# Top-k attention and a mixture-of-depths layer on one core: a software pipeline in another order

## The chip, the cores and the metric

The kernel runs on one core of one Trainium2 chip. The metric is the device time of one execution in microseconds. Five engines work side by side, each through its own list of instructions in order, and wait for each other by semaphores: TensorE (PE; its weight loads are PEld), VectorE (DVE), ScalarE (ACT), GpSimd (POOL) and SyncE (SP), which here only issues DMAs.

## What is computed

For 8 batches and 8 heads, 576 queries attend to 576 keys, but only to those whose score reaches the 32nd largest of the row. The result, 576 rows of 512 numbers per batch, is the input of the second part: the 128 rows with the largest gate pass through a small two-layer network and are added back.

```python
def _attn_ref(q, k, v):                      # (8, 8, 576, 64)
    scores = scale * np.matmul(q, k.transpose(0, 1, 3, 2))
    kth = np.partition(scores, -32, axis=-1)[..., -32:-31]
    scores = np.where(scores >= kth, scores, -1e9)
    attn = softmax(scores)
    return np.matmul(attn, v)

def _moe_ref(x, w_gate, w1, w2, capacity):   # x (8, 576, 512), capacity 128
    scores = np.einsum('bsd,d->bs', x, w_gate)
    out = x.copy()
    for b in range(B):
        top_idx = np.argpartition(-scores[b], capacity)[:capacity]
        xe = x[b, top_idx]
        ye = np.maximum(xe @ w1, 0.0) @ w2
        g = 1.0 / (1.0 + np.exp(-scores[b, top_idx]))
        out[b, top_idx] = x[b, top_idx] + g[:, None] * ye
    return out
```

## The kernel before

All is fp32. The work is cut into 160 units: 8 batches, 5 query tiles `t` (four of 128 rows, one of 64) and 4 head pairs `hp`. A unit of t=0 to 3 has two score tiles of 128 x 576, one per head; a unit of t=4 has one, with the 64 rows of both heads. One turn of the main loop, a step `n`, works on several units at once, each at another stage. The step's place within its batch is called i (n mod 20) below.

For a unit u the stages are these. In step u-1 TensorE multiplies its scores into PSUM (`multiply`, tile `ps`) and ScalarE copies them to `sc` (`keep`). In step u VectorE finds a lower bound of the 32nd score (`find_bound`: 16 maxima of eight over pieces, tile `cand`, then three rounds, tiles `best`), and ScalarE cuts it to a shorter number (`cut`, tile `seen`). In step u+1 ScalarE takes the Sign of score against bound (`part`, tile `sides`, with a count), POOL multiplies score and Sign and appends a few steps that depend on the count (`y`, `fill`), and VectorE finds the exact 32nd score in `y` (`find_kth`, tile `next8`, printed as `next`). In step u+2 the mask `less` is made, for the first tile by ScalarE, for the second by POOL. In step u+3 TensorE turns scores and adds a large negative number where the mask is set (`turn` into `ptr`, `turn_last` for the last 64 keys into a corner of the step's `ps`), and ScalarE takes exponentials (`pT`, `last`). In step u+4 TensorE multiplies with the values (`values`, tile `av`; the last column sums the weights) and ScalarE copies that out (`keep_values`, tile `xs`). Every fourth unit ends a query tile: VectorE inverts the sums (`invert`), one step later POOL normalises (`normalise`) and VectorE makes the gate (`gates`).

Two generators are moved on by one part at the end of each step. `load_kq` fetches and turns the keys and queries of the next batch (tile `tr`, its copies wait in `late` until the next `flush`). `mixture` is the second layer for the batch before: from i=4 on two steps turn the gates, five rank the rows by a comparison with all (`junk`) and mark which row has which slot (`pick`), one multiplies the marks with row number and gate (`extra_ps`), one gathers the 128 rows by DMA, then come their turning, three steps of products with w1 (`h_ps`), four with w2 (`y_ps`) and a scatter that adds. `ps_misc`, one PSUM bank, holds whatever of these is in flight.

What sets the order is the program's own text: the wrapper `InOrder` (lines 34 to 42) keeps each engine's instructions as they are written. `ps` has one buffer of four banks, `ptr` two of one, `av` and `ps_misc` one each. Because `turn_last` and the next score product share a `ps` buffer, that product follows the exponential of `last` (line 764) on ScalarE.

Of the kernel before, what the change touches and what calls it, by code (L numbers as in the profile page):

```python
# [10 lines left out]
ALU = mybir.AluOpType  # L11
# [34 lines left out]
def kernel(  # L46
# [50 lines left out]
    nc.gpsimd.iota(tok_i[:, J:NT], pattern=[[0, 1]], base=JP, channel_multiplier=1)  # L97
    slot_i = const.tile([P, CAP], I32, name="slot_i")
    nc.gpsimd.iota(slot_i, pattern=[[1, CAP]], base=0, channel_multiplier=0)
    slot = const.tile([P, CAP], FP32, name="slot")  # L100
# [391 lines left out]
    def mixture(row0, gate, rank, exact=False):  # L492
# [23 lines left out]
        extra = modpool.tile([P, NT, 2], FP32, name="extra")  # L516
        sig = modpool.tile([P, NT], FP32, name="sig")
        parts = ((slice(0, P), slice(0, J)), (slice(0, R), slice(J, NT)))
        for n, t in parts:
            dve.tensor_scalar_add(  # L520
                out=extra[n, t, 0],
                in0=tok_i[n, t],
                scalar1=row0 if isinstance(row0, float) else row0[n, :],
            )

            dve.tensor_scalar_max(out=sig[n, t], in0=gate[n, t], scalar1=-88.0)
        late.append(
            lambda: [
                act.activation(sig[n, t], sig[n, t], AF.Exp, scale=-1.0)
                for n, t in parts  # L530
            ]
        )


        pick = modpool.tile([P, NT, CAP], FP32, name="pick")
        for t in range(NT):
            yield
            n = R if t == J else P
            junk = modpool.tile([P, S], FP32, name="junk", tag="scratch")
            dve.tensor_scalar(  # L540
                out=junk[0:n, :],
                in0=gate_row[0:n, :],
                scalar1=gate[0:n, t : t + 1],
                scalar2=None,
                op0=ALU.is_gt,
                op1=ALU.add,
                accum_out=rank[0:n, t : t + 1],
            )
# [9 lines left out]
            if t == 0:  # L558
                for n, t in parts:
                    dve.tensor_scalar_add(out=sig[n, t], in0=sig[n, t], scalar1=1.0)  # L560
                    dve.reciprocal(out=extra[n, t, 1], in_=sig[n, t])

        yield
        ps = ps_misc.tile([P, 512], FP32, name="extra_ps", tag="misc")
# [12 lines left out]
        yield  # L577
        row_i = modpool.tile([P, 1], I32, name="row_i", bufs=2)
        done = B if exact else int(row0) // S + 1

        dve.tensor_scalar_min(out=row_i, in0=picked[:, 0:1], scalar1=float(done * S - 1))
# [21 lines left out]

        hT = modpool.tile([P, NFC, CAP], FP32, name="hT")
        for f0 in range(0, NFC, 3):
            yield
            fcs = range(f0, min(f0 + 3, NFC))
# [18 lines left out]
        for fc in range(NFC):  # L626
# [9 lines left out]
            lambda ps=ps: act.activation(gy, ps, AF.Copy, scale=picked[:, 1:2])  # L636
# [11 lines left out]
    def gates(t, x, gate):  # L648
        n = R if t == J else P
        prod = modpool.tile([P, S], FP32, name="prod", tag="scratch")  # L650
        dve.tensor_tensor_reduce(
            out=prod[0:n, 0:HD],
            in0=x[0:n, t, :],
            in1=wg[0:n, :],
            scale=1.0,
            scalar=0.0,
            op0=ALU.mult,
            op1=ALU.add,
            accum_out=gate[0:n, t : t + 1],
        )  # L660

# [14 lines left out]
    load_at = (3, 6, 7, 8, 9, 10, 12, 13, 14)  # L676
    first_load_at = (5, 6, 7, 8, 9, 10, 11, 12, 13)
    load_steps = {}
    for b in range(B - 1):
        at = [b * per_batch + i for i in (load_at if b else first_load_at)]  # L680
# [17 lines left out]
    scs, bests, next8s, masks, weights = {}, {}, {}, {}, {}  # L698
# [4 lines left out]
    for n in range(-1, len(units) + 6):  # L703
# [19 lines left out]
        if tiles_of(n - 3):  # L723
            sc, less, trs = scs.pop(n - 3), masks.pop(n - 3), []
            pT = ptpool.tile([P, 2, J, P], FP32, name="pT")
            last = ptpool.tile([P, P], FP32, name="last")
        if tiles_of(n - 4):
            b4, t4, hp4 = units[n - 4]
            av = ps_av.tile([P, 512], FP32, name="av")
        if tiles_of(n - 3) or tiles_of(n + 1):  # L730
            ps = room_for_scores()
        for i in range(2):
            if i < tiles_of(n - 3):
                trs.append(turn(i, sc, less))
                if i == tiles_of(n - 3) - 1:
                    trs.append(turn_last(i + 1, sc, ps, less))
            if i < tiles_of(n - 4):
                values(t4, hp4, i, *weights[n - 4], av, qkv[b4][2])


        if tiles_of(n):
            bests[n] = find_bound(tiles_of(n), scs[n])


        if tiles_of(n - 1):
            sides = wkpool.tile([P, 2, S], BF16, name="sides")
            y = wkpool.tile([P, 2, S + 8], FP32, name="y")
            for i in range(tiles_of(n - 1)):
                part(i, scs[n - 1], first_tile[n - 1], sides)
                pool.tensor_tensor(  # L750
                    y[:, i, 0:S], scs[n - 1][:, i, :], sides[:, i, :], ALU.mult
                )
            fill(tiles_of(n - 1), y, first_tile[n - 1])
            next8s[n - 1] = find_kth(tiles_of(n - 1), y)
        if tiles_of(n - 3):
            w = tiles_of(n - 3)
# [7 lines left out]
            act.activation(last[0 : w * R, :], trs[w], AF.Exp, scale=scale)  # L764
            weights[n - 3] = pT, last
        flush()
        if tiles_of(n + 1):
            b, t, hp = units[n + 1]
            multiply(t, hp, *qkv[b][0:2], ps)
        if tiles_of(n - 2):  # L770
            w, at = tiles_of(n - 2), first_tile[n - 2]
            kth = next8s.pop(n - 2)
            masks[n - 2] = mask(w, scs[n - 2], kth)
            pool.tensor_copy(out=seen[:, 1, at : at + w], in_=kth[:, 0:w, 7])
        if tiles_of(n - 4):
# [6 lines left out]
            weights.pop(n - 4)  # L782
            keep_values(t4, hp4, av, xs)
        if tiles_of(n + 1):
            scs[n + 1] = keep(tiles_of(n + 1), ps)
        if tiles_of(n):
            cut(tiles_of(n), bests.pop(n), first_tile[n])
# [13 lines left out]
        if b > 0 and i == mix_at:  # L801
# [13 lines left out]
    for _ in mixing:  # L815
        flush()
# [142 lines left out]
```

## Time and profile before

| | |
|---|---|
| median of 3 runs | 1075.84 us (1075.49 to 1076.65) |
| profiled execution | 1080.1 us, its span 1077.9 us |
| busy share of the span: TensorE, VectorE, ScalarE, POOL | 93%, 79%, 74%, 66% |
| mean granted clock of TensorE | 0.931 |
| chain that ended last, by engine | PE 62%, DVE 21%, ACT 9%, POOL 5% |

The profile is one execution. The granted clock is a share of 2.4 GHz; 0.50 is 1.2 GHz. A row of waits names who waited, and behind the arrow what ended the wait. The helper's line (L42) stands for nearly all instructions, so groups are told apart by their tiles.

### The profile page before, as it was taken

Reading aid. Unit: us, or ns where it says so; the run is one execution under the profiler, and the core shown is the slowest. Engines: PE = TensorE matmul, PEld = TensorE weight load, DVE = VectorE, ACT = ScalarE, POOL = GpSimd, SP = SyncE. Lnnn points to the kernel's source line nnn. Section 1 sums busy time; section 2 is a strip of 40 time slices with the busy share of each in tenths; the row PEclk is TensorE's granted clock in tenths of the full one; section 3 lists DMA queues with packets and bytes.
Section 4 is the critical chain, followed back from the end, with each engine's and each line's share of the span. In section 5 each row is a group of like instructions: output and inputs, shape, how many; then the busy total and the mean of one; then the engine's idle time right before and its main releaser. Section 6 shows DMA issues by size and latency. Waiting matters only on the chain.

```text
span 1077.9 us, 24886 instructions
## 1 busy us (share of the span) xinstructions
PE 1002.5 (93%) x7962; PEld 810.6 (75%) x7962; DVE 850.9 (79%) x4981; ACT 797.4 (74%) x1961; POOL 707.5 (66%) x814
## 2 busy tenths in 40 slices
PE   5899989999899999999999998999989999889966
PEld 3688778786778867787777877878677886777844
DVE  4999898868898689985888869896889858897440
ACT  4899788777787678885886868887788767777510
POOL 3788587664786557883776838786578655787410
PEclk9999999799897999899987999899989799888978
DMA  5741104100241003310131102320024000100020
GB/s 115 227 104 35 40 7 94 45 11 2 58 105 40 1 2 94 70 40 2 55 79 40 31 2 55 89 50 11 2 60 94 11 2 2 55 1 12 2 63 13
DMA packets 123834, 49.13 MB, mean 46 GB/s; under 512 B 118960, under 2 KB 118960, under 8 KB 122672
## 3 DMA queue, kind: packets, MB, share of 16 engines
q1 hardware_dynamic: 120320, 42.88, 15.5%
q0 software_dynamic: 1792, 4.20, 2.3%
q8 instruction: 65, 1.06, 0.4%
q14 instruction: 73, 0.60, 0.2%
q10 hardware_dynamic: 1584, 0.39, 0.2%
HBM read 35.91 MB, written 11.53 MB: 44 GB/s over the span
## 4 chain that ended last, share of the span: by engine, by line
PE 62%; DVE 21%; ACT 9%; POOL 5%; issue 2%; DMA 1%; SPq 0%; ACTq 0%; POOLq 0%
PE av L42 19%; PE ps L42 15%; PE ptr L42 12%; DVE cand L42 10%; PE h_ps L42 6%; PE y_ps L42 6%; DVE next L42 5%; POOL y L42 4%; ACT sides L42 3%; DVE best L42 2%; ACT sc L42 2%; PE tr L42 2%; DVE junk L42 2%; ACT pT L42 2%; PE extra_ps L42 1%
## 5 line engine op out<-in xcount | busy, mean ns | idle before, releaser
L42 POOL TENSOR_TENSOR y<-sc,sides 128x576 f32<-128x576 f32 x288 | 366.6, 1292 | 293.0 <-ACT sides L42 293.0
L42 DVE MAX8 cand<-sc 128x8 f32<-128x72 f32 x2304 | 323.8, 216 | 131.4 <-ACT sc L42 131.4
L42 PE MATMUL av<-v,pT 128*128 128x65 f32 (+1 forms) x2560 | 328.7, 274 | 0.0
L42 PEld LDWEIGHTS av<-v,pT 128*128 128x128 f32 (+1 forms) x2560 | 299.4, 189 | 8.4 <-issue 1.7
L42 PE MATMUL ps<-kT,qT 64*128 64x288 f32 (+1 forms) x1280 | 218.6, 464 | 29.0 <-ACT last L42 24.4
L42 PE MATMUL ptr<-ident,sc 128*128 128x128 f32 x1152 | 242.3, 290 | 0.0
L42 DVE MAX8 next<-y 128x8 f32<-128x584 f32 x288 | 207.3, 757 | 41.9 <-POOL y L42 38.9
L42 ACT COPY sc<-ps 128x576 f32<-128x576 f32 x288 | 172.0, 644 | 83.7 <-PE ps L42 81.9
L42 ACT ACTIVATE sides<-sc,seen 128x576 bf16<-128x576 f32 x288 | 221.2, 769 | 15.2 <-POOL seen L42 0.4
L42 ACT ACTIVATE pT<-ptr 128x512 f32<-128x512 f32 x288 | 159.1, 583 | 95.5 <-PE ptr L42 95.4
L42 PE MATMUL ptr<-out_of_reach,less 128*128 128x128 bf16 x1152 | 221.6, 226 | 1.9 <-POOL less L42 1.9
L42 POOL TENSOR_SCALAR less<-sc,next 128x576 bf16<-128x576 f32 x128 | 220.8, 1725 | 0.0
L42 PEld LDWEIGHTS ptr<-ident,sc 128*128 128x128 f32 x1152 | 175.6, 152 | 31.1 <-issue 16.2
L42 PEld LDWEIGHTS ps<-kT,qT 64*128 64x128 f32 (+1 forms) x1280 | 113.3, 192 | 78.5 <-ACT last L42 42.6
L42 DVE MAX8 best<-cand 128x8 f32<-128x64 f32 x864 | 154.2, 215 | 3.3
L42 PEld LDWEIGHTS <-less 128*128 128x128 bf16 (+1 forms) x1312 | 141.5, 108 | 15.1 <-issue 7.5
L42 ACT ACTIVATE less<-sc,next 128x576 bf16<-128x576 f32 x160 | 125.5, 784 | 0.0
L42 DVE MATCH_REPLACE8 cand<-best,cand 128x64 f32<-128x64 f32 x576 | 116.5, 209 | 0.0
L42 PEld LDWEIGHTS h_ps<-xeT,w 128*128 128x128 f32 x512 | 60.6, 196 | 11.8 <-ACT xs L42 9.2
L42 PE MATMUL h_ps<-xeT,w 128*128 128x128 f32 x512 | 65.2, 284 | 1.8 <-ACT hT L42 1.2
L42 PE MATMUL y_ps<-w,hT 128*128 128x512 f32 x128 | 62.6, 615 | 0.5 <-ACT hT L42 0.5
L42 ACT COPY xs<-av 128x130 f32<-128x130 f32 (+1 forms) x160 | 43.7, 273 | 24.2 <-PE av L42 24.1
(78 smaller groups left out, 919.6 us busy)
## 6 DMA issues: line engine op xcount, KB each, us to landing
rows<-in_k_dram SPq DMA_DIRECT2D x64, 128.0 KB, 2.9
v<-in_v_dram SPq DMA_DIRECT2D x64, 128.0 KB, 3.0
out_dram<-x SPq DMA_DIRECT2D x8, 1024.0 KB, 3.9
rows<-in_q_dram SPq DMA_DIRECT2D x62, 128.0 KB, 2.9
w<-in_moe_w_dram SPq DMA_DIRECT2D x2, 2048.0 KB, 14.1
last<-in_k_dram SPq DMA_DIRECT2D x8, 128.0 KB, 3.4
vlast<-in_v_dram SPq DMA_DIRECT2D x8, 128.0 KB, 3.3
vpair<-in_v_dram SPq DMA_DIRECT2D x16, 64.0 KB, 2.8
```

Of the source, the lines that this page charges most:

```text
L42: return lambda *a, **kw: self._tc.keep_in_program_order(fn(*a, **kw))
```

## The change

The order of a step is rewritten, and the second layer moves.

In a step `n`, TensorE first turns unit n-4, `last` before the two tiles, then multiplies the scores of n+1, then the values of n-4. ScalarE first takes the exponentials of n-4 (`last` first), then the loads' copies, the mask of n-3, the copies of the scores of n+1, the cut and the Signs of n-1, and the copy of the values at the end. VectorE finds the bound of n and then the 32nd score of n-2, whose `y` was made in the step before. Mask and turning thus come one step later for a unit; the values come at the step where they were.

On ScalarE a step with a load reads so before; the tiles are those named above, `kT` the loaded keys:

```order
L42 ACTIVATE sides,seen<-sc,seen 128x576 x2
L42 ACTIVATE pT<-ptr 128x512 x2
L42 ACTIVATE last<-ps 128x128
L42 COPY kT<-tr 128x512
L42 ACTIVATE less<-sc,next_6841 128x576
L42 COPY xs<-av 128x130
L42 COPY sc<-ps 128x576 x2
L42 CAST seen<-best_6908 128x2
```

and so after, from the exponentials of one step to the next step's first:

```order
L42 ACTIVATE last<-ps 128x128
L42 ACTIVATE pT<-ptr 128x512 x2
L42 COPY kT<-tr 128x512
L42 ACTIVATE less<-sc,next_6959 128x576
L42 COPY sc<-ps 128x576 x2
L42 CAST seen<-best_6932 128x2
L42 ACTIVATE sides,seen<-sc,seen 128x576 x2
L42 COPY xs<-av 128x130
```

The Signs moved from ahead of the exponentials to behind the copies, `last` ahead of `pT`, and the copy of the values to the end.

On TensorE a step of two tiles reads so before, around its end (`v` and `vpair` are the values, `rows` the keys being loaded):

```order
L42 MATMUL ps<-ident,sc 128x128
L42 LDWEIGHTS less
L42 MATMUL ps<-out_of_reach,less 128x128
L42 MATMUL av<-v_125,pT 128x65 x4
L42 MATMUL av<-vpair_129,last 128x130
L42 MATMUL ps<-kT,qT 128x288 x4
L42 MATMUL tr<-ident,rows 128x128 x4
L42 MATMUL ptr<-ident,sc 128x128
```

and so after, at the same place of a step, here the one that turns the last gate column:

```order
L42 MATMUL ptr<-ident,sc 128x128
L42 LDWEIGHTS less
L42 MATMUL ptr<-out_of_reach,less 128x128
L42 MATMUL ps<-kT,qT 128x288 x4
L42 MATMUL av<-v_132,pT 128x65 x8
L42 MATMUL av<-vpair_136,last 128x130
L42 MATMUL tr<-ident,gate 128x64
L42 MATMUL ps<-ident,sc 128x128
```

The score product moved from the end of the step to between turning and values, and the turning of `last` (`ps<-ident,sc`) to the start.

The mixture starts at i=8 instead of 4, and the loads at i=7 instead of 3. On VectorE, what stood behind the last gate of a batch (64 rows) before was this, with the first ranking one step later:

```order
L42 ISA prod,gate<-x,wg 64x512
L42 ISA gate 64x1
L42 TENSOR_SCALAR extra<-tok_i 128x4
L42 TENSOR_SCALAR sig<-gate 128x4
L42 TENSOR_SCALAR extra<-tok_i 64x1
L42 TENSOR_SCALAR sig<-gate 64x1
L42 MAX cand<-sc 128x8 x16
```

and after, with the first ranking five steps later:

```order
L42 ISA prod,gate<-x,wg 64x512
L42 ISA gate 64x1
L42 MAX cand<-sc 128x8 x16
L42 MAX best_4394<-cand 128x8 x2
L42 MATCH_REPLACE cand<-best_4394,cand 128x64 x2
```

The small work on gates went out of this place. The chosen rows' numbers now come from one product of bf16 marks with a constant table `place` of row numbers, split in two columns that bf16 holds exactly; the gates of the chosen rows are made again from the gathered rows by `dot`. The seventh batch's mixture ends in the drain of the pipeline with two parts a step, and the last batch's runs by itself at the end.

```diff
-    slot = const.tile([P, CAP], FP32, name="slot")
+    slot = const.tile([P, CAP], BF16, name="slot")
...
-        pick = modpool.tile([P, NT, CAP], FP32, name="pick")
+        pick = modpool.tile([P, NT, CAP], BF16, name="pick")
...
                 pick[0:n, t, :],
-                extra[0:n, t, :],
+                place[0:n, t, :],
...
+        g = modpool.tile([P, 1], FP32, name="g")
+        dot(P, xe, g)
+        dve.tensor_scalar_max(out=g, in0=g, scalar1=-88.0)
+        late.append(lambda: act.activation(g, g, AF.Exp, scale=-1.0))
...
-    load_at = (3, 6, 7, 8, 9, 10, 12, 13, 14)
-    first_load_at = (5, 6, 7, 8, 9, 10, 11, 12, 13)
+    load_at = (7, 10, 11, 12, 13, 14, 16, 17, 18)
...
-    mix_at = 4
+    mix_at = 8
...
+        if tiles_of(n - 4) or tiles_of(n + 1):
+            ps = room_for_scores()
+        if tiles_of(n - 4):
+            w, sc, less = tiles_of(n - 4), scs.pop(n - 4), masks.pop(n - 4)
+            tr_last = turn_last(w, sc, ps, less)
+            trs = [turn(i, sc, less) for i in range(w)]
             pT = ptpool.tile([P, 2, J, P], FP32, name="pT")
             last = ptpool.tile([P, P], FP32, name="last")
...
+            act.activation(last[0 : w * R, :], tr_last, AF.Exp, scale=scale)
...
         flush()
         if tiles_of(n + 1):
             b, t, hp = units[n + 1]
             multiply(t, hp, *qkv[b][0:2], ps)
+        if tiles_of(n - 3):
+            w, at, kth = tiles_of(n - 3), first_tile[n - 3], next8s.pop(n - 3)
+            masks[n - 3] = mask(w, scs[n - 3], kth)
+            pool.tensor_copy(out=seen[:, 1, at : at + w], in_=kth[:, 0:w, 7])
+        if tiles_of(n + 1):
+            scs[n + 1] = keep(tiles_of(n + 1), ps)
+        if tiles_of(n - 4):
+            b4, t4, hp4 = units[n - 4]
+            av = ps_av.tile([P, 512], FP32, name="av")
+            for i in range(tiles_of(n - 4)):
+                values(t4, hp4, i, pT, last, av, qkv[b4][2])
+
+
+        if tiles_of(n):
+            bests[n] = find_bound(tiles_of(n), scs[n])
         if tiles_of(n - 2):
...
+            next8s[n - 2] = find_kth(tiles_of(n - 2), ys.pop(n - 2))
+
+
+        if tiles_of(n - 1):
+            w, at, sc = tiles_of(n - 1), first_tile[n - 1], scs[n - 1]
+            cut(w, bests.pop(n - 1), at)
...
         next(mixing, None)
+        if n >= len(units):
+            flush()
+            next(mixing, None)
...
     for _ in mixing:
+        flush()
+    for _ in mixture(float((B - 1) * S), of_batch[B - 1][1], ranks[:, B - 1, :]):
         flush()
```

## Rows read from the trace of the kernel before

**Rows 1.** Windows: length; busy us (instructions) of each engine; clock; DMA; GB/s.

```profile
42.00:1012.69 970.69, 929.24 (x7550) 759.84 (x7546) 809.79 (x4755) 759.63 (x1875) 676.34 (x766) 0.94 0.17 41
```

**Rows 2.** Windows of single steps, two disturbed stretches, a batch, six batches.

```profile
344.89:350.36 5.47, 5.43 (x49) 4.65 (x49) 5.47 (x37) 5.35 (x14) 4.54 (x6) 1.00 0.21 48
107.01:111.88 4.87, 4.87 (x45) 4.00 (x44) 3.81 (x19) 4.08 (x10) 4.65 (x6) 1.00 0.01 3
350.36:355.66 5.30, 5.30 (x48) 4.43 (x49) 4.56 (x25) 5.21 (x14) 4.96 (x6) 1.00 0.01 3
282.31:297.95 15.64, 13.70 (x93) 11.31 (x93) 13.43 (x85) 11.07 (x29) 9.65 (x11) 0.78 0.12 27
308.89:339.43 30.54, 28.83 (x199) 24.07 (x199) 25.93 (x160) 21.48 (x53) 21.18 (x23) 0.78 0.19 44
191.81:205.46 13.65, 13.65 (x65) 10.87 (x62) 9.60 (x62) 6.67 (x17) 9.15 (x11) 0.50 0.07 19
247.03:377.11 130.08, 125.33 (x997) 101.94 (x996) 105.69 (x620) 99.50 (x245) 87.58 (x99) 0.92 0.18 43
121.29:888.77 767.48, 736.25 (x5956) 602.04 (x5955) 634.00 (x3721) 595.89 (x1469) 523.87 (x594) 0.93 0.17 42
```

**Rows 3.** Timeline of TensorE: start, us, what; idle before it and what ended that.

```profile
155.65 0.24 PE L42 MATMUL tr<-ident,gate 64*128 64x64 f32 x1 [2.06 <-DVE sig L42]
...
191.46 1.03 PE L42 MATMUL ps<-kT,qT 64*128 64x288 f32 x4 [1.45 <-ACT last L42]
```

**Rows 4.** Timeline of one undisturbed step without loads, late in the last batch.

```profile
981.28 1.24 PE L42 MATMUL ps<-kT,qT 64*128 64x288 f32 x8 [0.48 <-ACT last L42]
...
982.57 1.18 ACT L42 COPY sc<-ps 128x576 f32<-128x576 f32 x2 [0.52 <-PE ps L42]
...
983.93 0.78 ACT L42 ACTIVATE sides<-sc,seen 128x576 bf16<-128x576 f32 x1
...
984.95 2.52 POOL L42 TENSOR_TENSOR y<-sc,sides 128x576 f32<-128x576 f32 x2 [0.68 <-ACT sides L42]
...
985.47 1.06 ACT L42 ACTIVATE pT<-ptr 128x512 f32<-128x512 f32 x2
...
986.42 0.27 ACT L42 ACTIVATE last<-ps 128x128 f32<-128x128 f32 x1
986.58 0.78 ACT L42 ACTIVATE less<-sc,next 128x576 bf16<-128x576 f32 x1
...
986.75 1.24 PE L42 MATMUL ps<-kT,qT 64*128 64x288 f32 x8 [0.48 <-ACT last L42]
...
987.43 0.22 POOL L42 TENSOR_TENSOR y<-steps,seen 128x16 f32<-128x16 f32 x1
```

**Rows 5.** Timeline of VectorE and of POOL in a step with ranking.

```profile
311.33 1.42 DVE L42 MAX8 next<-y 128x8 f32<-128x584 f32 x2
312.67 0.67 DVE L42 CUSTOM_DVE_ANT_0 prod<-x,wg 128x512 f32<-128x512 f32 x1
...
313.38 0.81 DVE L42 TENSOR_SCALAR_CACHE_REDUCE junk<-gate_row,gate 128x576 f32<-128x576 f32 x1
...
314.49 2.24 DVE L42 MAX8 cand<-sc 128x8 f32<-128x72 f32 x16
...
318.20 0.75 DVE L42 MAX8 next<-y 128x8 f32<-128x584 f32 x1
...
312.75 2.97 POOL L42 TENSOR_TENSOR y<-sc,sides 128x576 f32<-128x576 f32 x2 [0.66 <-ACT sides L42]
...
315.88 1.72 POOL L42 TENSOR_SCALAR less<-sc,next 128x576 bf16<-128x576 f32 x1
```

**Rows 6.** Groups of instructions: shapes, count, busy us, mean ns of one, idle before.

```profile
L42 POOL TENSOR_TENSOR x<-xs,rden 128x512 f32<-128x512 f32 (+1 forms) x40 | 42.0, 1049 | 19.5 <-DVE rden L42 19.3
L42 PE MATMUL extra_ps<-extra,pick 128*128 128x2 f32 (+1 forms) x80 | 18.6, 344 | 3.9 <-DVE pick L42 2.0 <-DVE sig L42 1.9
L42 DVE TENSOR_SCALAR sums<-xs 128x8 f32<-128x8 f32 (+1 forms) x40 | 9.1, 228 | 11.3 <-ACT xs L42 11.3
```

More of the change, by code (lines that the diff above doesn't have):

```diff
@@ L97 @@
     nc.gpsimd.iota(tok_i[:, J:NT], pattern=[[0, 1]], base=JP, channel_multiplier=1)
+    place_i = const.tile([P, NT, 2], I32, name="place_i")
+    nc.gpsimd.iota(
+        place_i[:, 0:J, 0], pattern=[[0, J]], base=0, channel_multiplier=J
+    )
+    nc.gpsimd.iota(place_i[:, J:NT, 0], pattern=[[0, 1]], base=JP, channel_multiplier=0)
+    nc.gpsimd.iota(
+        place_i[:, 0:J, 1], pattern=[[1, J]], base=0, channel_multiplier=0
+    )
+    nc.gpsimd.iota(place_i[:, J:NT, 1], pattern=[[0, 1]], base=0, channel_multiplier=1)
+    place = const.tile([P, NT, 2], BF16, name="place")
+    nc.vector.tensor_copy(out=place, in_=place_i)
     slot_i = const.tile([P, CAP], I32, name="slot_i")
     nc.gpsimd.iota(slot_i, pattern=[[1, CAP]], base=0, channel_multiplier=0)
-    slot = const.tile([P, CAP], FP32, name="slot")
+    slot = const.tile([P, CAP], BF16, name="slot")
     nc.vector.tensor_copy(out=slot, in_=slot_i)
@@ L514, in mixture @@
         late.append(lambda tr=tr: act.copy(out=gate_row[:, JP:S], in_=tr[:, 0:R]))
[L516 to L532, printed above, removed]
-        pick = modpool.tile([P, NT, CAP], FP32, name="pick")
+        pick = modpool.tile([P, NT, CAP], BF16, name="pick")
         for t in range(NT):
@@ L557, in mixture @@
             )
[L558 to L561, printed above, removed]
         yield
-        ps = ps_misc.tile([P, 512], FP32, name="extra_ps", tag="misc")
+        ps = ps_misc.tile([P, 512], FP32, name="place_ps", tag="misc")
         for t in range(NT):
@@ L577, in mixture @@
         yield
+        row = modpool.tile([P, 1], FP32, name="row")
+        dve.scalar_tensor_tensor(
+            out=row,
+            in0=picked[:, 0:1],
+            scalar=row0 if isinstance(row0, float) else row0[:, 0:1],
+            in1=picked[:, 1:2],
+            op0=ALU.add,
+            op1=ALU.add,
+        )
         row_i = modpool.tile([P, 1], I32, name="row_i", bufs=2)
         done = B if exact else int(row0) // S + 1
-        dve.tensor_scalar_min(out=row_i, in0=picked[:, 0:1], scalar1=float(done * S - 1))
+        dve.tensor_scalar_min(out=row_i, in0=row, scalar1=float(done * S - 1))
         xe = modpool.tile([P, HD], FP32, name="xe", tag="gy")
@@ L606, in mixture @@
             yield
+            if f0 == 3:
+                dve.tensor_scalar_add(out=g, in0=g, scalar1=1.0)
+                dve.reciprocal(out=g, in_=g)
             fcs = range(f0, min(f0 + 3, NFC))
@@ L646, in mixture, with dot @@
         )
-    def gates(t, x, gate):
-        n = R if t == J else P
+    def dot(n, x, g):
         prod = modpool.tile([P, S], FP32, name="prod", tag="scratch")
@@ L652, in gates @@
             out=prod[0:n, 0:HD],
-            in0=x[0:n, t, :],
+            in0=x,
             in1=wg[0:n, :],
@@ L658, in gates @@
             op1=ALU.add,
-            accum_out=gate[0:n, t : t + 1],
+            accum_out=g,
         )
+    def gates(t, x, gate):
+        n = R if t == J else P
+        dot(n, x[0:n, t, :], gate[0:n, t : t + 1])
     def store(ob, x):
@@ L673 @@
     per_batch = NT * NHP
-    load_at = (3, 6, 7, 8, 9, 10, 12, 13, 14)
-    first_load_at = (5, 6, 7, 8, 9, 10, 11, 12, 13)
+    load_at = (7, 10, 11, 12, 13, 14, 16, 17, 18)
     load_steps = {}
     for b in range(B - 1):
-        at = [b * per_batch + i for i in (load_at if b else first_load_at)]
+        at = [b * per_batch + i for i in load_at]
         load_steps[at[0] - 1] = b + 1, True
@@ L697 @@
     of_batch = {}
-    scs, bests, next8s, masks, weights = {}, {}, {}, {}, {}
+    scs, bests, ys, next8s, masks = {}, {}, {}, {}, {}
     def tiles_of(n):
@@ L720 @@
             normalising = None
-        if tiles_of(n - 3):
-            sc, less, trs = scs.pop(n - 3), masks.pop(n - 3), []
+        if tiles_of(n - 4) or tiles_of(n + 1):
[4 more added lines that the diff above has]
+            trs = [turn(i, sc, less) for i in range(w)]
             pT = ptpool.tile([P, 2, J, P], FP32, name="pT")
             last = ptpool.tile([P, P], FP32, name="last")
[L727 to L756, printed above, removed]
+            act.activation(last[0 : w * R, :], tr_last, AF.Exp, scale=scale)
             for i in range(w):
@@ L763 @@
                 )
-            act.activation(last[0 : w * R, :], trs[w], AF.Exp, scale=scale)
-            weights[n - 3] = pT, last
         flush()
@@ L769 @@
             multiply(t, hp, *qkv[b][0:2], ps)
-        if tiles_of(n - 2):
[L771 to L774, printed above, removed]
+        if tiles_of(n - 3):
[11 more added lines that the diff above has]
+            bests[n] = find_bound(tiles_of(n), scs[n])
+        if tiles_of(n - 2):
+            next8s[n - 2] = find_kth(tiles_of(n - 2), ys.pop(n - 2))
+        if tiles_of(n - 1):
+            w, at, sc = tiles_of(n - 1), first_tile[n - 1], scs[n - 1]
+            cut(w, bests.pop(n - 1), at)
+            sides = wkpool.tile([P, 2, S], BF16, name="sides")
+            y = wkpool.tile([P, 2, S + 8], FP32, name="y")
+            for i in range(w):
+                part(i, sc, at, sides)
+                pool.tensor_tensor(y[:, i, 0:S], sc[:, i, :], sides[:, i, :], ALU.mult)
+            fill(w, y, at)
+            ys[n - 1] = y
         if tiles_of(n - 4):
@@ L800 @@
         b, i = divmod(n, per_batch)
-        if b > 0 and i == mix_at:
+        if 0 < b < B and i == mix_at:
             mixing = mixture(float((b - 1) * S), of_batch[b - 1][1], ranks[:, b - 1, :])
         next(mixing, None)
+        if n >= len(units):
+            flush()
+            next(mixing, None)
         if n in load_steps:
```

7 lines of the change are left out of this document (1 added, 6 removed).

## The prediction

> **What bounds the kernel now.** I read four views, in this order. First the busy times of the long middle stretch, from 42 us to the last score product: TensorE is busy 929.2 of 970.7 us, VectorE 809.8 and ScalarE 759.6, and TensorE's mean clock is 0.94 [rows 1]. So what counts is where TensorE stands still, 41.5 us in all, or runs at its lower clock. Second, the same view step by step (a step is one turn of the main loop; i is its number within the 20 of a batch, and the row of a step starts with its score product). An undisturbed step takes 5.47 us at clock 1.00, with ScalarE busy 5.35 and VectorE 5.47. Two stretches of each batch are not like that: 15.64 us where two undisturbed steps would be 10.94, and 30.54 us where four would be 21.88, both at a mean clock of 0.78, and in the second a piece of 13.65 us at 0.50 with TensorE busy all the time [rows 2]. So of the 130.1 us of this batch 4.7 + 8.7 = 13.4 are such disturbance. The six batches from 121.29 us on take 767.5 us, 127.9 each [rows 2], 2.2 less than this one, and I put the mean disturbance at 13.4 - 2.2 = 11.2 us: 4.6 for the first stretch, 6.6 for the second, over seven batches 78 us.
>
> Third, TensorE's own order of time at the two places. The first begins with 2.06 us idle before the turning of the last gate column, ended by VectorE; the second with 1.45 us before a score product, ended by ScalarE's `last` [rows 3]. Behind each the granted clock goes to 1.2 GHz. Shorter waits do not do that: a step without loads has 0.48 us before the same product [rows 4] again and again, and the undisturbed steps stand at 1.00 [rows 2].
>
> Fourth, one undisturbed step. The score product waits for ScalarE's exponential of `last`, which stands behind two Signs and two exponentials; those stand behind the copies of the previous scores. Product start 981.28, copies 982.57, Signs 983.93, exponentials 985.47, `last` 986.42, next product 986.75: a ring of 5.47 us through ScalarE, with 0.48 us idle on TensorE where no loads fill it [rows 4]. TensorE alone needs less: 4.87 us in a step at 107.01 us and 5.30 in one with four turnings more at 350.36 us, both without any idle time [rows 2].
>
> **The change part by part.** The sum is made against the profiled execution: span 1077.9, 1080.1 with what lies around it, and that is 4.3 above the median of the runs, 1075.84.
>
> *The gate column (mixture four steps later).* The mixture turns the gates at i=4 and 5, and the last gate is made by VectorE at the end of step 5: TensorE must wait for the whole of VectorE's step. After, the turnings stand at i=8 and 9, three steps behind that gate. Wait and low clock go: -4.6 us a batch. What is late next at i=5 and 6 is the products with w2, which now stand there; that is TensorE's own work, moved and not added. VectorE's 5.1 to 5.8 us lie beneath these steps, which hold 4.87 us and the products.
>
> *The ring (turning, next scores, values; exponentials first).* `last` is turned first and its exponential is first on ScalarE, so the product no longer waits for Signs. What is left is throughput: ScalarE's instructions by their starts, `last` 0.16, two exponentials 0.95, mask 0.67, copies and cut 1.36, two Signs 1.54 [rows 4], and with xs and a load's copy 5.35 in all [rows 2]; TensorE 5.30. The values' exponentials finish under the 1.24 us product. So 5.35 where it was 5.47, in about 12 steps a batch: -1.4 us.
>
> *The 32nd score a step later.* VectorE needs 3.71 us for the bound (314.49 to 318.20) and 1.34 for the 32nd scores (311.33 to 312.67) [rows 5], 5.05 of 5.35. Counted from a score product at 0: copies start at 2.1, the bound runs from 2.7 to 6.4, the Signs begin at 3.5, POOL's y (2.52 and 0.22) ends at 7.0, the 32nd scores end at 8.35, and ScalarE's mask that needs them stands at 1.45 of two steps on, 12.15. POOL's mask would start at 12.35. So VectorE may be late by 4.5 to 4.9 us before anyone waits. Today that reserve is small: the cut that follows the bound stands at the end of the same step, and so the rank steps end in the 1.45 us of idle TensorE of [rows 3].
>
> *The rank steps, i=10 to 14.* Each adds 1.11 us to VectorE (313.38 to 314.49), i=9 and 13 a gate product of 0.71 [rows 5], i=8 and 12 a denominator and its reciprocal, about 0.46 (two such as [rows 6]). Less the 0.3 us that each step has over (step 9, without a load, has none), the lag grows to 0.7, 1.5, 2.3, 3.2, 4.5, 6.0, 6.8 from i=8 to 14. It passes the reserve in the last two: two waits of about 1.1 and 0.8 us, 1.9 together, in place of the second stretch's 6.6: -4.7 us. Queued behind the waiting mask on ScalarE are the next copies, the cut and the Signs; TensorE's next product waits for the copies' place. I take it that neither wait brings the clock down, since 1.45 did and 0.48 did not; this is the step of which I am least sure, and both ends are kept: 0 and 6.6.
>
> *POOL.* `last` needs the mask of both tiles, and the second is POOL's 1.72 us. Its chain (y 2.74, mask 1.72) ends at 8.75 from the product; the turning stands at 5.35 + 3.8 = 9.1. Where the normalisation (1.05 us [rows 6]) lies between, POOL is 0.6 late: in three steps a batch outside the long ones, +1.6 us. From below it is 0, if ScalarE sets the pace anyway.
>
> In the rank steps POOL's two y took 2.97 us, with VectorE's gate product and the picks beside them [rows 5], where they take 2.52 otherwise [rows 4]. The Trainium skill (SBUF — State Buffer, Who interferes with whom) says that VectorE and GpSimd share a port pair which the one locks for a whole instruction, also when VectorE works in a two-port mode or with two SBUF inputs. The row agrees, 0.45 us in one step; by that rule the bf16 picks and the added product for the chosen rows still lock it, and 0.45 in five rank steps of seven batches would make the time 16 us longer, an estimate from these rows.
>
> *Slots' rows by bf16.* Ten passes become five per batch. The old ones are 18.6 us over 8 batches, 2.3 each, mostly at the low clock [rows 6]; at full clock half of the passes should be near 0.6, and the part that is not in the second stretch already I put at -0.5. Ten small VectorE instructions go, six small ones and one 0.7 us product for the 128 rows come, that at i=19 where VectorE has one tile only: 0.
>
> *Ends.* The seventh mixture runs two parts per drain step, with a copy between them on the path: +3 us. The last mixture is a serial tail as before.
>
> Sum: -4.6 - 1.4 - 4.7 + 1.6 - 0.5 = -9.6 a batch, times 7 = -67, plus 3: span 1013.9, run 1016.1, median 4.3 lower: 1012.
>
> **Rivals.** (1) *The clock falls once a batch still*, because the wait at i=14 comes out over 1.4 us (a reserve smaller by 0.5 is enough, since a step with rank and gate product exceeds its time by 1.5). For it: the sizes lie close. Against it: the excess is split in two. The second stretch stays as dear as now: 4.7 x 7 = 33 more, 1045. (2) *No new waits*: the reserve holds, POOL is hidden: 1.6 + 1.9 less a batch, 987. (3) *Slower*: the mask on ScalarE, waiting for VectorE, holds up the copies which VectorE itself needs next, so that each rank step from i=12 stops everybody, with the low clock after each. A wait with its low clock is worth 6.6 us today; three a batch make 19.8 against 11.2 now: +8.6 x 7 = +60, less 2 for the rest, 1133. It decides from a mean of 1.7 such waits a batch on, which needs a reserve under 2 us instead of 4.5. (4) *No difference*: the ring is replaced by another of the same length (turning, exponentials, values, xs, turning) and the waits move: 1076. Against it: its members sum to under 5 us by the rows.
>
> **Chances.** Forecast 0.50, (1) 0.30, (2) 0.09, (3) 0.06, (4) 0.05; what the ports may cost lies between forecast and (1). Range 984 to 1050: from (2) to just over (1). A measurement of this kernel tells 0.2%, 2 us, from no change; faster 0.90, the same 0.03, slower 0.07.
>
> **What would show it.** In the profile after: undisturbed steps with loads of 5.3 to 5.4 us; no wait of TensorE for VectorE before the gates' turning; at i=0 to 6 longer steps with TensorE never idle; ScalarE's `less` waiting for VectorE's `next` only at i=15 and 16; small waits of TensorE for POOL's `less`. It is wrong if clock pieces of 1.2 GHz remain in every batch, if steps with loads take over 5.5 us, or if TensorE waits for `pT` in each step.

## The result and the profile after

The changed kernel takes 1048.05 us (median of 4 runs, 1047.36 to 1048.25) where 1075.84 was: ratio 0.974 [0.9723, 0.9756]. The forecast was 1012; the time lies inside the range of 984 to 1050, but only 28 of the 64 us came.

The windows of the changed kernel, columns as in [rows 2]: three steps and an undisturbed one, a half-clock piece, five batches, the stretch from the first score product of the second batch to the last of all, and what follows it:

```profile
304.60:309.95 5.35, 5.35 (x51) 4.62 (x49) 5.24 (x25) 5.09 (x14) 4.69 (x6) 1.00 0.01 2
298.61:304.60 5.99, 5.43 (x46) 4.33 (x46) 5.99 (x38) 5.76 (x14) 5.99 (x8) 1.00 0.00 0
332.13:338.67 6.54, 5.44 (x51) 4.25 (x50) 6.50 (x41) 5.02 (x13) 4.59 (x6) 1.00 0.13 30
344.72:352.68 7.96, 5.47 (x50) 4.35 (x49) 7.23 (x37) 4.37 (x11) 6.82 (x9) 1.00 0.11 33
226.38:236.62 10.24, 10.24 (x53) 7.90 (x50) 5.16 (x24) 4.63 (x11) 3.48 (x6) 0.50 0.00 1
236.56:848.24 611.68, 587.18 (x4951) 468.69 (x4950) 536.72 (x3088) 503.25 (x1220) 433.26 (x495) 0.99 0.19 46
120.29:963.43 843.14, 804.84 (x6764) 642.00 (x6762) 747.29 (x4289) 693.25 (x1684) 602.67 (x688) 0.98 0.17 42
963.43:1046.20 82.77, 55.44 (x364) 40.41 (x362) 21.28 (x88) 19.85 (x49) 13.95 (x17) 0.85 0.11 26
```

The undisturbed step takes the 5.35 us forecast, but TensorE is busy for all of it, and ScalarE for 5.09. Five batches take 122.3 us each where six took 127.9 [rows 2]: 5.6 less, forecast 9.6. Three kinds of step are longer than TensorE's work, and the 7.96 us one is the worst. The last row, from the last score product to the end, is 82.8 us long; before it was 65.2 (span 1077.9 less the end of [rows 1]).

TensorE's timeline in one batch, its waits only:

```profile
336.22 0.17 PE L42 MATMUL place_ps<-place,pick 64*128 64x2 bf16 x1 [0.61 <-DVE pick L42]
...
337.14 0.23 PE L42 MATMUL ps<-out_of_reach,less 128*128 128x128 bf16 x1 [0.49 <-POOL less L42]
...
343.19 0.23 PE L42 MATMUL ps<-out_of_reach,less 128*128 128x128 bf16 x1 [0.58 <-POOL less L42]
...
351.15 0.23 PE L42 MATMUL ps<-out_of_reach,less 128*128 128x128 bf16 x1 [2.49 <-POOL less L42]
```

The wait for the last gate [rows 3] is gone. In its place TensorE waits for VectorE's last pick and, at the turning of `last`, for POOL's mask; these are steps i=15 to 17. At i=9 and 13 there are two more waits for the mask, of 0.56 and 0.39. Why the last is so long is seen on POOL, in the same batch:

```profile
343.22 1.28 POOL L42 TENSOR_TENSOR y<-sc,sides 128x576 f32<-128x576 f32 x1
345.85 1.07 POOL L584 DMA_INDIRECT xe<-out_dram,row_i  x1 [1.34 <-DVE row_i L42]
346.93 1.30 POOL L42 TENSOR_TENSOR y<-sc,sides 128x576 f32<-128x576 f32 x1
348.18 0.22 POOL L42 TENSOR_TENSOR y<-steps,seen 128x16 f32<-128x16 f32 x1
348.35 1.04 POOL L42 TENSOR_TENSOR x<-xs,rden 128x512 f32<-128x512 f32 x1
349.37 1.72 POOL L42 TENSOR_SCALAR less<-sc,next 128x576 bf16<-128x576 f32 x1
```

The gather of the chosen rows moved with the mixture from i=12 to i=16 and stands between the two tiles' y: POOL waits 1.34 us for `row_i`, which VectorE makes late, and spends 1.07 on issuing. The normalisation follows, then the mask. The clock falls behind this wait in four of the seven batches. In the third it falls behind the waits at i=15, in the last behind a wait of 1.6 us for the mask at i=13, and the second has no half-clock piece.

ScalarE's waits for `next` in the same batch:

```profile
334.53 0.78 ACT L42 ACTIVATE less<-sc,next 128x576 bf16<-128x576 f32 x1 [1.22 <-DVE next L42]
...
340.58 0.78 ACT L42 ACTIVATE less<-sc,next 128x576 bf16<-128x576 f32 x1 [1.15 <-DVE next L42]
```

These are the two waits forecast for i=15 and 16, of about 1.1 and 0.8.

### The profile page after: what moved, and what is told of

It reads as the page before. It is cut to its first block, busy times and chain, and to the rows that moved or that the text cites. A ratio compares the mean times of both kernels' runs of the same rounds, so it can differ in the third digit from the quotient of the medians.

```text
span 1046.2 us, 24796 instructions
## 1 busy us (share of the span) xinstructions
PE 961.1 (92%) x7922; PEld 761.8 (73%) x7922; DVE 867.1 (83%) x4966; ACT 807.5 (77%) x1953; POOL 702.6 (67%) x818
## 4 chain that ended last, share of the span: by engine, by line
PE 53%; DVE 27%; POOL 10%; ACT 6%; issue 3%; DMA 1%; SPq 0%; POOLq 0%; ACTq 0%; DVEq 0%
PE av L42 16%; DVE cand L42 12%; PE ps L42 12%; PE ptr L42 11%; PE h_ps L42 6%; DVE next L42 6%; PE y_ps L42 5%; POOL less L42 4%; POOL y L42 4%; DVE best L42 3%; DVE junk L42 2%; DVE pick L42 2%; PE tr L42 2%; ACT sc L42 2%; POOL x L42 1%
## 5 line engine op out<-in xcount | busy, mean ns | idle before, releaser
L42 PEld LDWEIGHTS av<-v,pT 128*128 128x128 f32 (+1 forms) x2560 | 275.2, 182 | 69.5 <-issue 25.4
L42 PE MATMUL av<-v,pT 128*128 128x65 f32 (+1 forms) x2560 | 301.8, 269 | 2.8 <-ACT pT L42 2.8
L42 PE MATMUL ptr<-ident,sc 128*128 128x128 f32 x1152 | 222.9, 286 | 0.0
L42 ACT ACTIVATE pT<-ptr 128x512 f32<-128x512 f32 x288 | 169.8, 597 | 57.9 <-PE ptr L42 48.6
L42 PE MATMUL ptr<-out_of_reach,less 128*128 128x128 bf16 x1152 | 211.5, 223 | 0.0
L42 PE MATMUL ps<-kT,qT 64*128 64x288 f32 (+1 forms) x1280 | 206.3, 442 | 5.4 <-ACT qT L42 2.7
L42 PEld LDWEIGHTS ptr<-ident,sc 128*128 128x128 f32 x1152 | 165.6, 144 | 16.8
L42 PEld LDWEIGHTS ps<-kT,qT 64*128 64x128 f32 (+1 forms) x1280 | 107.1, 182 | 55.0 <-issue 25.5
L42 ACT ACTIVATE last<-ps 128x128 f32<-128x128 f32 (+1 forms) x160 | 43.7, 273 | 77.6 <-PE ps L42 76.8
L42 PE MATMUL ps<-out_of_reach,less 128*128 128x128 bf16 (+1 forms) x160 | 36.6, 229 | 35.7 <-POOL less L42 35.3
L42 PEld LDWEIGHTS h_ps<-xeT,w 128*128 128x128 f32 x512 | 61.4, 198 | 4.9 <-ACT hT L42 2.4
```

The costliest lines, as they stand in the source:

```text
L42: return lambda *a, **kw: self._tc.keep_in_program_order(fn(*a, **kw))
```

## The experiments

The stretch from the second batch's first score product to the last product, split into TensorE's idle time, half of its busy time in pieces at 1.2 GHz (loss, an estimate), and the rest (work), from the profiles:

| kernel | stretch us | work | idle | loss | after it |
|---|---|---|---|---|---|
| before | 891.4 | 790.3 | 39.7 | 61.4 | 65.2 |
| after | 843.1 | 789.6 | 38.3 | 15.3 | 82.8 |
| later gather | 818.6 | 789.5 | 22.7 | 6.3 | 89.7 |
| and gate products late | 807.8 | 788.3 | 18.2 | 1.3 | 88.7 |
| and normalisation late | 804.0 | 788.4 | 13.9 | 1.7 | 88.7 |

The windows of the first row and of the fourth that are not shown elsewhere:

```profile
121.29:1012.69 891.40, 851.75 (x6859) 694.48 (x6858) 736.58 (x4325) 686.76 (x1694) 609.88 (x690) 0.93 0.16 38
1012.69:1077.90 65.21, 45.00 (x280) 32.16 (x279) 15.63 (x66) 14.35 (x37) 9.68 (x12) 0.83 0.13 32
124.90:932.72 807.82, 789.61 (x6765) 634.79 (x6763) 745.01 (x4285) 691.72 (x1684) 602.63 (x686) 1.00 0.18 43
```

Work is the same throughout, within 2 us. From before to after nearly the whole gain in the stretch is in the clock, and the idle time of before was replaced, not removed. The theory: POOL's queue (gather and normalisation ahead of the mask) and VectorE's lag in the rank steps make the new waits. In the expectations a wait is counted by the row that starts with its score product, one above the code's step; edits are counted by the code's step.

**The gather two steps later.**

```diff
         late.append(lambda ps=ps: act.copy(out=picked, in_=ps[:, 0:2]))
         yield
+        yield
+        yield
         row = modpool.tile([P, 1], FP32, name="row")
...
         yield
-        yield
-        yield
         xeT = modpool.tile([P, NDC, CAP], FP32, name="xeT")
```

> The gather of the chosen rows is issued two steps later (i=18, where no POOL mask stands behind it) and the two empty steps behind it fall away. Theory (POOL's queue): in the 7.96 us step at i=18 the mask on POOL is late because the gather stands ahead of it, 1.34 us waiting for row_i and 1.07 us issuing; so TensorE's wait of 2.49 us falls to 0 to 0.3 in every batch, the half-clock pieces behind it go (10.2 us of loss in seven batches), about 3.9 us a batch: 1018 to 1024 us. Rival (VectorE's lag): the mask is late because its 32nd scores are late, the gather only fills that time; TensorE still waits over 1.5 us there, 1042 to 1048 us.

Measured: 1031.98 us, 0.9592 [0.9546, 0.9637]. POOL in the former 7.96 us step, and that step:

```profile
575.79 2.52 POOL L42 TENSOR_TENSOR y<-sc,sides 128x576 f32<-128x576 f32 x2
578.28 0.21 POOL L42 TENSOR_TENSOR y<-steps,seen 128x16 f32<-128x16 f32 x1
578.66 1.04 POOL L42 TENSOR_TENSOR x<-xs,rden 128x512 f32<-128x512 f32 x1 [0.17 <-DVE rden L42]
579.68 1.72 POOL L42 TENSOR_SCALAR less<-sc,next 128x576 bf16<-128x576 f32 x1
```

```profile
577.29:582.99 5.70, 5.47 (x51) 4.35 (x49) 5.49 (x21) 4.38 (x11) 5.53 (x7) 1.00 0.01 3
121.99:940.55 818.56, 795.85 (x6764) 637.22 (x6762) 748.61 (x4287) 692.90 (x1684) 604.29 (x686) 0.99 0.17 42
```

The mask follows y without the gather, TensorE's 2.49 became 0.23, and the stretch is 24.6 us shorter: the theory, 3.5 us a batch of the 3.9 expected. The rival is refuted. The time fell by 16 only, less than the theory's 24 to 30, since 6.9 us came back behind the stretch and the start was 1.7 longer. What came back is the edit's own: the seventh mixture's gather now stands one step ahead of its rows' turning instead of three, that step has no score product, and TensorE waits for the rows to land, with a half-clock piece of 10.2 us behind the wait.

```profile
950.49 0.66 PE L42 MATMUL xe_ps<-ident,xe 128*128 128x128 f32 x4 [2.73 <-DMA xe<-out_dram,row_i]
```

The runs below that keep this edit keep this cost (the last column of the table).

**The normalisation behind the mask.** The block with `normalise` moves behind `pool.tensor_copy(out=seen[:, 1, ...])`.

> The normalisation on POOL is issued behind the mask of its step instead of ahead of it. Theory (POOL's queue): the waits of 0.56 and 0.39 us in the steps at i=10 and 14 go, the one of 2.49 at i=18 falls by the 1.04 us of the normalisation to about 1.45; 2.0 us a batch and some or all of the low clock behind it, 1024 to 1034 us. Rival: the delay is only handed on, to y, the 32nd scores and the mask of the next step; waits of the same size stand one step later, 1045 to 1050 us.

Measured: 1034.53, 0.9616 [0.9567, 0.9666]. The 0.56 went and the 2.49 became 1.50, as the theory had it, but 0.38 and 0.65 stand in the two steps where 0.39 and 0.06 were: the rival is right in the rank steps. Idle time in the stretch fell from 38.3 to 31.7 only; most of the gain is the clock (loss 5.1 for 15.3), which the wait of 1.50 does not bring down here, though waits of 1.45 did in the kernel before.

**The 32nd scores first.**

```diff
+        early = n > per_batch and n % per_batch in range(13, 18)
+        if early and tiles_of(n - 2):
+            next8s[n - 2] = find_kth(tiles_of(n - 2), ys.pop(n - 2))
         if tiles_of(n):
             bests[n] = find_bound(tiles_of(n), scs[n])
-        if tiles_of(n - 2):
+        if not early and tiles_of(n - 2):
```

> In the steps i=13 to 17 VectorE takes the 32nd scores ahead of the next unit's bound. Theory (VectorE's lag of the rank steps holds the masks): ScalarE's waits for next of 1.22 and 1.15 us in the steps at i=16 and 17 go and TensorE's 0.49 and 0.58 for POOL's mask with them; the 0.61 for the last pick stays, and so does the 2.49 at i=18, which is the gather's: 1.1 us a batch, about 1040 us. Rival (the bound is as urgent): the cut and the Signs come later by the 1.3 us, y with them, and the waits move on by a step or two: 1046 to 1052 us.

Measured: 1042.38, 0.9669 [0.9607, 0.9731]. The two waits of 0.49 and 0.58 went (0.10 is left), the 0.61 for `pick` grew to 0.90, and 2.33 of the 2.49 stayed: the steps i=15 to 17 of an inner batch stand still 3.3 us instead of 4.2, 0.85 less where the theory had 1.1. The masks were held by VectorE's order, but part of the time turned up again at the pick.

**The three together.**

> The three edits together. Theory: of the 4.73 us that TensorE stands still in an interior batch only the 0.61 for the last pick is left, and no half-clock piece: about 4.1 + 1.5 a batch, 1006 to 1012 us. Rival (TensorE is bounded by another ring, so that waits move to other places): 1020 us or more, with waits of over 0.3 us in steps that had none.

Measured: 1038.01, 0.9645 [0.9596, 0.9694], slower than the later gather alone. The rival won; TensorE's timeline:

```profile
574.40 0.17 PE L42 MATMUL place_ps<-place,pick 64*128 64x2 bf16 x1 [2.60 <-DVE pick L42]
```

The waits of the rank steps were gathered in one, for VectorE's last pick, and the clock falls behind it.

**And the products for the chosen rows a step later.** `yield` twice ahead of `place_ps`, once less behind it; the load of i=16 at 15.

> As the three edits together, and the products for the chosen rows (place_ps) a step later, at i=16, with the load step of i=16 at 15. Theory: the 2.60 us in which TensorE waited there for VectorE's last pick go, and with them the half-clock piece behind each; an interior batch falls from 119.5 to about 117.2 us, where TensorE is busy nearly throughout: 1012 to 1020 us. Rival (VectorE's lag is on the path wherever the ranks end): a wait of 1 us or more for pick, row_i or next stands at i=16 to 18 in every batch: 1028 us or more.

Measured: 1033.2 (1029.9 to 1043.88, the last of which was profiled), 0.9596 [0.9566, 0.9627]. The rival's verdict, by a wait that neither had named: ScalarE's cut waits for VectorE's bound, and TensorE's product behind it for `last`.

```profile
570.12 0.19 ACT L42 CAST seen<-best 128x2 f32<-128x2 bf16 x1 [2.67 <-DVE best L42]
```

```profile
572.35 2.05 PE L42 MATMUL ps<-kT,qT 64*64 64x288 f32 x8 [1.91 <-ACT last L42]
```

With the later gather alone the waits of i=15 to 17 sum to 0.61 + 0.49 + 0.58 + 0.23 = 1.9 us; here it is one wait of 1.9. Whoever is served first on VectorE, the sum does not fall (it was 2.6 in the three together): it is VectorE's excess of work there.

**The old places of the mixture in the new order.** `mix_at = 4` and the loads' steps of before.

> The changed kernel with the mixture and the loads at their old steps (mixture at i=4). Theory (the gate column's wait came from the mixture's place, 4.6 us a batch): TensorE waits about 2 us for the last gate at i=5 again and the clock falls behind it: 4.6 x 7 = 32 us more, less about 6 for the drain, 1065 to 1080 us. Rival (the new order by itself gave the gate more time, the place of the mixture matters little): under 1052 us.

Measured: 1081.8, 1.0073 [1.0039, 1.0107]: 0.7% slower than before. TensorE and POOL in one batch:

```profile
541.19 0.34 PE L42 MATMUL tr<-ident,gate 64*128 64x64 f32 x1 [4.27 <-DVE gate L42]
...
592.11 0.29 PE L42 MATMUL ps<-out_of_reach,less 128*128 128x128 bf16 x1 [4.88 <-POOL less L42]
```

```profile
585.58 1.07 POOL L584 DMA_INDIRECT xe<-out_dram,row_i  x1 [3.79 <-DVE row_i L42]
```

The gate's wait is there, twice as long as expected, and the gather's too: issued at i=12, among full steps, it holds POOL for 3.79 us until `row_i` is there, and TensorE waits 4.88 for the mask a step later. It is a second dose of the gather; the rival is refuted.

**The mixture four steps later in the old order.** `mix_at`, `load_at` and the drain of the changed kernel, all else as before.

> The kernel before with only the mixture and the loads moved four steps on and two parts of it in each drain step. Theory: the gate column's wait and low clock go, 4.6 x 7 = 32 us less; the drain grows by the first products moved into it, about 6 to 8: 1048 to 1056 us. Rival (the wait is handed to another place of the old order, whose ring leaves no room): 1070 us or more.

Measured: 1079.04 (1071.16 to 1084.58), 1.0024 [0.9991, 1.0056]: no difference. The gates' turnings wait for nobody, yet ScalarE and TensorE at i=11 have this:

```profile
569.31 0.19 ACT L42 CAST seen<-best 128x2 f32<-128x2 bf16 x1 [2.46 <-DVE best L42]
```

```profile
572.40 0.82 PE L42 MATMUL ps<-kT,qT 64*128 64x288 f32 x2 [2.60 <-ACT last L42]
```

The rival: the stretch is 18.9 us shorter in this profile (its fastest run) than before, but a wait of 2.60 us stands in the rank steps instead of the gate's 2.06, and the time behind the last product grew by 10. The old order needs the cut in the step of its bound, so VectorE's lag ends there. Neither part of the change made the kernel faster alone; here the time behind the last product took back a part of what the stretch gained.

**`last` between the tiles.**

```diff
-            tr_last = turn_last(w, sc, ps, less)
-            trs = [turn(i, sc, less) for i in range(w)]
+            trs = [turn(0, sc, less)]
+            tr_last = turn_last(w, sc, ps, less)
+            trs += [turn(i, sc, less) for i in range(1, w)]
```

> The last columns are turned between the two tiles instead of ahead of both. Theory (they expose POOL's mask, which both tiles' last columns need): 0.68 us more for that mask in each step; the waits of 0.56, 0.39, 0.49 and 0.58 us go, the 2.49 falls to about 1.8: up to 2.7 us a batch, 1028 to 1036 us, if ScalarE can begin its exponentials 0.68 later. Rival (ScalarE's ring still sets the step): it is busy 5.2 to 5.3 of 5.35 us, so the steps with loads grow to 5.6 us or more, 0.3 in about 12 steps a batch, 25 us more, which eats the gain: 1045 to 1060 us.

Measured: 1050.69, 0.9769 [0.9738, 0.98]. The waits for the mask at i=9 and 13 went, as the theory has it, but those of i=15 to 17 stayed (1.03, 0.56, 2.49). The rival's place was wrong, its sign right: two-tile steps stay at 5.35, while in one-tile steps, where `last` now comes at the very end, the product waits:

```profile
486.24 1.24 PE L42 MATMUL ps<-kT,qT 64*128 64x288 f32 x8 [0.36 <-ACT last L42]
```

**Two gate products out of the rank steps** (on top of the later gather).

```diff
-            gates(t, *of_batch[b])
+            gb, t = gating
+            if t > 1:
+                gates(t, *of_batch[gb])
...
+        if 0 <= b < B and i in (18, 19):
+            gates(i - 18, *of_batch[b])
```

> On top of the later gather: VectorE's gate products of the first two row tiles move from i=9 and 13 to i=18 and 19, where it has one tile only. Theory (what is left at i=15 to 18 is VectorE's lag, one sum of 1.9 us a batch that moves but keeps its size whatever the order): 1.5 us less work ahead of the ranks' end takes 1.5 of the 1.9 away; the normalisation's 0.56 and 0.39 stay: 1.5 x 7 = 10 us less than with the later gather alone, 1020 to 1024 us. Rival (the waits come from the order of the queues, not from VectorE's total): they stay as they are, 1030 to 1034 us.

Measured: 1020.85, 0.9479 [0.9444, 0.9515]. Only the 0.56 at i=16 and 0.23 at i=17 are left of the 1.9, an interior batch takes 117.6 us for 119.2, and no half-clock piece is left in the five inner batches: the theory, in place and in the time. Of the 1.9 us 1.1 went where 1.5 was expected; of the 10.8 us by which the stretch is shorter 5.0 are the clock's.

**And the normalisation late.**

> The same with the normalisation behind the mask on POOL. Theory: without a lag on VectorE the later y is hidden, and 0.56 and 0.39 go too: 0.9 x 7 = 6 us less again, 1014 to 1018 us. Rival (the delay is handed on to the 32nd scores, as 0.38 and 0.65 at i=14 and 15 were when it was tried alone): no gain, 1020 to 1026 us.

Measured: 1015.18 (1013.66 to 1015.69), 0.9434 [0.9399, 0.9469], the fastest but for the next, which it equals. An interior batch and the stretch:

```profile
460.60:577.78 117.18, 115.79 (x993) 93.28 (x991) 107.07 (x619) 100.10 (x245) 87.02 (x100) 1.00 0.20 48
119.03:923.04 804.01, 790.13 (x6764) 635.16 (x6762) 740.79 (x4284) 689.34 (x1684) 602.34 (x685) 1.00 0.18 43
```

The time is the theory's, the mechanism half so: the waits at i=9 and 13 went, but 0.49 stands again at i=15. The stretch is 3.8 us shorter, not 6; the rest of the profiled difference is a start 5.9 us shorter. TensorE is now busy 790 of 804 us.

**And the 32nd scores first at i=15 to 17.**

> The same with the 32nd scores ahead of the bound at i=15 to 17. If VectorE's lag by then is under what masks and Signs have in reserve, no order of the two makes a difference: within 3 us of the run without it. If the order of the queue matters still: 3 us or more off, either way.

Measured: 1014.0, 0.9429 [0.9392, 0.9466]: no difference, as expected once the lag is within the reserve.

**One part of the mixture in each drain step** (on the changed kernel).

> The changed kernel with one part of the seventh mixture in each drain step instead of two; what is left of it comes behind the last step, ahead of the last mixture. The forecast put the pairs at 3 us, for a copy on the path between their halves. Theory: the products are the path whichever way they are paired, and the copies' waits of 0.5 to 0.8 us only change place: within 3 us of the changed kernel, 1045 to 1051 us. Rival (the pairs are what made the drain 17 us longer): 1036 to 1042 us.

Measured: 1047.08, 0.9732 [0.9696, 0.9769]: no difference in the time, against the rival. But the equal times do not show the theory. In the profile what follows the last score product is 5.3 us shorter than the 82.8 of the changed kernel:

```profile
967.57:1045.06 77.49, 53.79 (x364) 39.43 (x362) 18.61 (x71) 19.64 (x49) 13.45 (x17) 0.88 0.11 27
```

The stretch, whose program is the same, lost 21.6 us to the clock instead of 15.3, and began 1.6 later. Whether the other runs hide the 5.3 us in the same way is open.

## Why the prediction was wrong

*The gate column* held: its wait is gone. That it is worth 4.6 us by itself did not: alone it gave nothing that could be told from before, and in the new order the old place cost 34 us, gate and gather together: 44 more in the stretch, 6.3 a batch, and 10 less behind it. The sum counted each part as if the others were done.

*The ring* held in size, 5.35 in the undisturbed steps, but not in its limit: ScalarE's 5.35 was to set it, and TensorE's own work does. That the two forecasts lay 0.05 apart made the number right.

*The rank-step waits* held in place and size: two waits of ScalarE, 1.22 and 1.15 us, and TensorE stands still 1.68 at i=15 and 16 where 1.9 was forecast. But it waits for the last pick and for POOL's mask, not for the copies behind ScalarE's. And the size is in part luck: by its own terms the lag comes to about 6.1 us at i=14, not 6.8, the reserve to 4.4 to 4.6, not 4.5 to 4.9, and what POOL adds to the picks (see the ports) was not in it. That this time is VectorE's, and that no order tried with the later gather brought it under 1.9, the runs showed.

*POOL* is the step that failed. Its chain was counted as y, mask and, "where the normalisation lies between", 0.6 us "in three steps a batch". Two of the three are so (0.56 and 0.39). The third, i=17, also has the gather, which moved with the mixture and which the sum left out, though its issue and its wait for `row_i` both stand in POOL's queue ahead of the mask that TensorE now needs first: 2.49 us, and the clock behind it. Taking the gather out shortened the stretch by 24.6 us, to 818.6; the forecast for it was 891.4 - 67 = 824. The term was priced at 1.6 us a batch; the two small waits cost 0.95, and the gather 24.6 / 7 = 3.5.

Of the 36 us between forecast and measured time, 18.7 lie in the stretch (843.1 for 824.4), less than the gather cost: the other terms together came out 6 better than forecast. The ends make 14.5. Another 4 come from taking off 4.3 us for the step from profile to median, which is 0.2 here, and the start was 1 us shorter.

*The clock* was forecast not to fall in the rank steps. The loss went from 61 to 15 us. The changed kernel's time is nearly that of rival (1), 1045, and the clock did fall, but 10.2 of the 15.3 us behind another wait than that rival's: the gather's. The rest is in part the rival's. In the third batch the clock fell behind the rank-step waits, and with the gather out of the way it did so in three batches, so that neither wait brings the clock down did not hold either. With the later gather 6 us were left, and 1.3 once the lag was smaller.

*The ports.* In the rank steps y took 2.52 us again, not the 2.97 of [rows 5]: POOL did not pay, VectorE did. In the last mixture, with POOL idle, a pick takes 0.25 us; of the five picks of one inner batch four took longer:

```profile
308.69 0.93 DVE L42 TENSOR_SCALAR pick<-slot,ranks 128x128 bf16<-128x128 bf16 x1
315.43 1.15 DVE L42 TENSOR_SCALAR pick<-slot,ranks 128x128 bf16<-128x128 bf16 x1
322.87 0.45 DVE L42 TENSOR_SCALAR pick<-slot,ranks 128x128 bf16<-128x128 bf16 x1
329.86 0.74 DVE L42 TENSOR_SCALAR pick<-slot,ranks 128x128 bf16<-128x128 bf16 x1
...
1008.09 0.25 DVE L42 TENSOR_SCALAR pick<-slot,ranks 128x128 bf16<-128x128 bf16 x1
```

```profile
314.01 2.52 POOL L42 TENSOR_TENSOR y<-sc,sides 128x576 f32<-128x576 f32 x2 [1.20 <-ACT sides L42]
...
328.57 1.98 POOL L42 TENSOR_SCALAR less<-sc,next 128x576 bf16<-128x576 f32 x1 [0.81 <-DVE next L42]
```

Each of the four ended 0.05 us after a POOL instruction that ran beside it: y, y, the normalisation, and the mask, which took 1.98 us instead of 1.72. That is 2.3 us more of VectorE's time in the rank steps of a batch, as much as the 0.45 in five steps from which the 16 us were worked out. The lock that the Trainium skill (SBUF — State Buffer, Who interferes with whom) describes for VectorE in a two-port mode, where the later of the two stands still until the other's end, agrees with these ends. What it cost the kernel was not tried by itself.

*Slots' rows* held. The group of all eight mixtures, where 18.6 us was [rows 6]:

```profile
L42 PE MATMUL place_ps<-place,pick 128*128 128x2 bf16 (+1 forms) x40 | 3.8, 168 | 8.5 <-DVE pick L42 8.5
```

*The ends* were mis-sized: 17.5 us more behind the last score product, not 3. By the windows of before and after, 10.4 of it is TensorE's work: the first layer of the seventh mixture, moved there from the stretch, and a pipeline one step longer. The other 7.1 are idle, 4.7 of them in the drain: with no score product beneath them the exponentials are waited for, 0.7 us four times, and copies of the mixture, 0.5 to 0.8. Most of the rest is in the last mixture, where TensorE waits 3.19 us for the last gate instead of 2.30, and longer for its picks. The pairs, to which the 3 us were put, made 5.3 by the profile with one part a step. With the mixture at its old place in the new order 72.6 us follow the last score product, so its later place makes 10. How much of these 17.5 us can be had back in the time is not shown.

## What to carry to other kernels

When a step is moved, list each queue in which it stands, with what is ahead and behind it there, the DMA issues of a compute engine among them: such an issue holds its engine from its first wait on, and everything behind it waits for the one number it lacks. An engine that has more work than time in some steps makes others wait; here, with the gather out of the way, reordering chose who waited and how much at once, and only work taken out of these steps made the sum smaller. Parts of a change that free the same engine are not to be priced one by one.

## What the runs showed of the hardware

In two profiles a single longer wait cost more than nearly the same time in pieces. In the three together and in the later gather alone TensorE's stretch idles 25.4 and 22.7 us, but the first, with its 2.60 us at one place, has a half-clock piece behind that wait in every batch and loses 15.5 us, the second 6.3. The stretch of the three together:

```profile
121.05:949.18 828.13, 802.76 (x6764) 641.97 (x6763) 748.57 (x4287) 690.23 (x1684) 604.59 (x685) 0.98 0.17 42
```

Short waits are no safe side. With the later gather alone no wait of an inner batch is over 0.61 us, and yet the clock fell behind those of 0.61 and 0.49 at i=15:

```profile
687.91 0.17 PE L42 MATMUL place_ps<-place,pick 64*128 64x2 bf16 x1 [0.61 <-DVE pick L42]
688.84 0.29 PE L42 MATMUL ps<-out_of_reach,less 128*128 128x128 bf16 x1 [0.49 <-POOL less L42]
```

```profile
688.20:691.59 3.39, 2.90 (x18) 2.05 (x17) 3.39 (x29) 2.00 (x7) 3.36 (x5) 0.50 0.00 0
```

It did so in two of the five inner batches. With the gates and the normalisation late, with no wait over 0.58 us there, the five inner batches show no half-clock piece at all.

VectorE's gate product took 2.11 us, where 0.67 is usual [rows 5], when it met POOL's y, in the new order with the mixture's old place:

```profile
538.93 2.11 DVE L42 CUSTOM_DVE_ANT_0 prod<-x,wg 64x512 f32<-64x512 f32 x1
```

```profile
537.96 2.50 POOL L42 TENSOR_TENSOR y<-sc,sides 128x576 f32<-128x576 f32 x2
540.43 0.68 POOL L42 TENSOR_TENSOR y<-steps,seen 128x16 f32<-128x16 f32 x1
```

It ended 0.6 us after y's two tiles were done, about its usual time behind them. The 1.4 us that this adds are part of the 4.27 us for which TensorE waited there for the gate.
